# Fused attention and two MLPs on one core: the sum of the last exponential tiles, the scaling, the reciprocals and the first two weights are placed anew

## The chip, the core and the metric

The kernel runs on one core of a Trainium2 chip. Its engines work side by side, each through its own queue in order: TensorE (PE, with its weight loads shown as PEld), VectorE (DVE), ScalarE (ACT), GpSimd (POOL), and SyncE (SP), which here issues loads and stores. The metric is the device time of one execution in microseconds; times of before and after are medians over runs.

## The reference, cut to what matters

```
q_pool = q.reshape(B, H, S // 2, 2, D).mean(axis=3)          # B=2 H=8 S=1152 D=64
scores = matmul(q_pool, k^T) / sqrt(D)
scores = scores - max(scores); attn = exp(scores)
attn   = attn / (sum(attn) + 1e-9)
x = (attn @ v)                      # as 1152 tokens x 512
h = x @ w_in (512 x 2048);  g = relu(h)^2;  y = g @ w_out
out = ((y @ w_a) * (y @ w_b)) @ w_out2                        # 512 x 1536, 512 x 1536, 1536 x 512
```

The weights come as 64-bit words and are taken apart into two float32 parts each (hi and lo), and activations likewise, so that each product of the MLPs is three matmuls (hi hi, hi lo, lo hi).

## The kernel before

The program has a manual schedule: each engine does its instructions in the order in which the code issues them, and only data and buffers make it wait.

**Attention** runs in 16 units (`NU`); unit n is a pair of heads p = n // 2 and half c = n % 2 of its 576 pooled queries, 288 columns (`CQ`). The loop over n (L481) issues for each unit: nine score tiles (`scores`, L365: eight matmuls into a PSUM tile, and an ACT exponential into `e`), and between them, as the letters of `ORDER` say, six steps of the row maxima of the next pair (`max_pair`, L317: a matmul pair into PSUM and a DVE reduction `mm`); behind an odd unit the mixed maxima (`px`) and the negated maxima (`max_end`, `nmw`); the transposes of the pair after that (`prep`, with a copy on ACT to `hi` and the rest on DVE to `lo`); the maxima as a row (`max_row`); then `values` (L399, 36 passes on PE into `po`, copied by ACT to `xf`) and the denominator of the unit before (`denom`, L409: the sums of exponentials `acc` times ones on PE, ACT writes `sg`). Scores, maxima, transposes, values and denominators share four PSUM tiles of two banks (`two_banks`) in turn, so a matmul of the next unit can wait for a DVE reduction to give a tile back.

The sum of a unit's nine exponential tiles: POOL adds tiles 0 to 6 one after the other into `acc` (L382, L384), DVE adds 7 and 8 (`sum_last`, L393), and POOL adds that at the start of the next unit (`sum_end`, L397). Two units later DVE takes the reciprocal of `sg` and scales `xf` by it (`scale`, L426 to L430), both right after the sum of tiles 7 and 8; one unit later ACT and POOL split `xf` (`x_split`, L432) into `xh` and `xl`, the input of the first MLP. The last unit sums its tiles 4 to 8 on DVE (L389).

**Weights** are made in three stages per tile of 512 x 128 (`w_stage`, L121): stage 0 an ACT copy (`wa`) and a DVE operation (L131), stage 1 two DVE operations (L135, L138), stage 2 a subtraction `wlo` (L153) on DVE or, for i from `NE` to 11, on POOL; ACT copies `whi` (L119) before it. Before the change the first `NE` = 4 weights are made in units 12 to 15, three steps in each (L519 to L521), and the first MLP starts with four early tiles (`early_mm`, f = 0 to 3, over the 576 tokens of the first batch, in the PSUM tiles of attention), which lie between the last values and the split of the last unit. Then the other half of the tokens follows for these f in tiles of 288, and f from `NE` on in three tiles of 384 (`mlp1`).

## Time and profile before

| | |
|---|---|
| median of 3 runs | 667.69 us (666.58 to 667.91) |
| profiled execution: its own time / its span | 666.69 us / 664.9 us |
| PE busy | 648.3 us, 98% |
| DVE, ACT, POOL busy | 455.9, 306.2, 203.0 us |
| attention, first values to first tile of the MLP | 30.34 to 234.02 us |
| mean granted clock of TensorE | 0.983 |

Busy shares are over the whole span, and POOL's work lies nearly all in attention, where it is busy nine tenths of the time. Matmuls are pipelined, so a row's duration is longer than the distance to the next; where PE waits is read from its idle time and from the start times. For the attention it helps to cut the span at the first value matmul of each unit, since every unit has the same work in between, but for the maxima (none in units 14 and 15, which have no next pair) and the transposes (none from unit 12 on).

### The profile page before, as it was taken

The page shows a single profiled execution, that of the slowest core. Times are in us where ns is not written, and L with a number is a line of the kernel's source. Part 1 is how long each engine was busy: PE and PEld are TensorE (multiplying, and loading weights), DVE is VectorE, ACT ScalarE, POOL GpSimd, SP SyncE. Part 2 cuts the span into 40 slices and gives each one's busy share as a digit, 9 for nine tenths or more (in the row PEclk, how much of TensorE's full clock was granted, in tenths as well). Part 3 has the DMA queues.
Part 4 walks back from the last instruction along what each step waited for, and adds up shares of the span by engine and source line. Part 5 has one row for each costly group of instructions (what it writes and reads, how often), then busy time and mean ns, then how long its engine had stood idle before and what let it go on. Part 6 is the DMA issues. An engine that isn't in the chain of part 4 may idle for free.

```text
span 664.9 us, 11353 instructions
## 1 busy us (share of the span) xinstructions
PE 648.3 (98%) x4618; PEld 584.5 (88%) x4618; DVE 455.9 (69%) x700; ACT 306.2 (46%) x571; POOL 203.0 (31%) x160
## 2 busy tenths in 40 slices
PE   7999999999979999999999999999999999999997
PEld 5878777777757789999999999999999889999986
DVE  7778988978998898982458855676777112777211
ACT  1546665575554746742356632244554222455100
POOL 1677999999975911310000000000000000000000
PEclk8799999999998999999999999999999999999999
DMA  8704404221041112422333222233434210341022
GB/s 198 159 1 108 100 9 107 53 57 37 4 146 33 47 33 66 126 96 63 96 91 101 94 65 64 64 127 96 128 127 126 65 32 3 125 127 63 18 65 63
DMA packets 55541, 52.90 MB, mean 80 GB/s; under 512 B 20416, under 2 KB 49344, under 8 KB 55488
## 3 DMA queue, kind: packets, MB, share of 16 engines
q1 hardware_dynamic: 55280, 51.58, 27.4%
q8 instruction: 36, 0.59, 0.4%
q10 hardware_dynamic: 208, 0.59, 0.3%
q14 instruction: 17, 0.14, 0.1%
HBM read 49.81 MB, written 2.36 MB: 78 GB/s over the span
## 4 chain that ended last, share of the span: by engine, by line
PE 83%; DVE 12%; ACT 2%; issue 1%; POOL 1%; DVEq 0%; POOLq 0%; ACTq 0%
PE ps L372 9%; PE y L559 5%; PE y L557 5%; PE y L558 5%; PE h L559 4%; PE h L557 4%; PE h L558 4%; PE po L403 4%; PE a L559 4%; PE a L558 4%; PE b L559 4%; PE b L558 4%; PE a L557 4%; PE b L557 4%; PE o L559 4%; PE o L557 4%
## 5 line engine op out<-in xcount | busy, mean ns | idle before, releaser
L384 POOL TENSOR_TENSOR acc<-acc,e 128x576 f32<-128x576 f32 x77 | 113.6, 1475 | 10.2 <-ACT e L377 4.2
L315 DVE TENSOR_REDUCE mm<-pm 128x2 f32<-128x768 f32 x96 | 88.8, 954 | 19.7 <-PE pm L323 19.0
L377 ACT ACTIVATE e<-ps 128x576 f32<-128x576 f32 x144 | 88.3, 656 | 27.7 <-PE ps L372 25.6
L153 DVE TENSOR_TENSOR wlo<-wx,whi 128x512 fp32r<-128x512 f32 x60 | 41.2, 687 | 54.3 <-ACT whi L119 54.2
L403 PE MATMUL po<-e,vin 128*64 128x288 f32 x576 | 73.3, 409 | 0.0
L119 ACT CAST whi<-wx 128x512 fp32r<-128x512 f32 x68 | 42.1, 620 | 64.3 <-DVE wx L138 64.3
L557 PE MATMUL y<-gh,whi 128*128 128x384 f32 x192 | 64.6, 336 | 0.0
L559 PE MATMUL y<-gh,wlo 128*128 128x384 f32 x192 | 64.5, 336 | 0.0
L558 PE MATMUL y<-gl,whi 128*128 128x384 f32 x192 | 64.5, 336 | 0.0
L403 PEld LDWEIGHTS po<-e,vin 128*64 128x64 f32 x576 | 40.0, 137 | 26.4 <-issue 0.2
L559 PE MATMUL h<-xh,wlo 128*128 128x384 f32 (+1 forms) x176 | 57.5, 327 | 0.0
L558 PE MATMUL h<-xl,whi 128*128 128x384 f32 (+1 forms) x176 | 57.5, 327 | 0.0
L557 PE MATMUL h<-xh,whi 128*128 128x384 f32 (+1 forms) x176 | 57.5, 327 | 0.0
L372 PE MATMUL ps<-hi 64*128 64x288 f32 x288 | 48.2, 329 | 6.8 <-DVE mm L315 6.5
L700 DVE TENSOR_TENSOR t<-b,as 128x384 f32<-128x384 f32 x36 | 20.1, 558 | 46.2 <-PE b L559 46.2
L138 DVE SCALAR_TENSOR_TENSOR wx<-raw,wx 128x512 int32<-128x512 int32 x68 | 49.7, 731 | 2.4
L135 DVE SCALAR_TENSOR_TENSOR wx<-wa,wx 128x512 int32<-128x512 int32 x68 | 48.3, 711 | 0.0
L559 PE MATMUL a<-yh,wlo 128*128 128x384 f32 x144 | 48.1, 334 | 0.0
L557 PE MATMUL a<-yh,whi 128*128 128x384 f32 x144 | 48.1, 334 | 0.0
L558 PE MATMUL a<-yl,whi 128*128 128x384 f32 x144 | 48.1, 334 | 0.0
L557 PE MATMUL b<-yh,whi 128*128 128x384 f32 x144 | 48.1, 334 | 0.0
L558 PE MATMUL b<-yl,whi 128*128 128x384 f32 x144 | 48.1, 334 | 0.0
(111 smaller groups left out, 1564.1 us busy)
## 6 DMA issues: line engine op xcount, KB each, us to landing
raw<-in_moe_w_out_dram SPq DMA_DIRECT2D x28, 512.0 KB, 3.4
raw<-in_moe_w_in_dram SPq DMA_DIRECT2D x16, 512.0 KB, 3.8
raw<-in_moe_w_a_dram SPq DMA_DIRECT2D x12, 512.0 KB, 3.5
raw<-in_moe_w_b_dram SPq DMA_DIRECT2D x12, 512.0 KB, 3.6
vin<-in_v_dram SPq DMA_DIRECT2D x8, 576.0 KB, 4.2
qin<-in_q_dram SPq DMA_DIRECT2D x7, 576.0 KB, 5.6
kin<-in_k_dram SPq DMA_DIRECT2D x14, 288.0 KB, 5.8
out_dram<-oacc SPq DMA_DIRECT2D x5, 192.0 KB, 2.2
```

Source lines behind the costliest of these rows:

```text
L119: nc.scalar.copy(w["hi"], w["x"].bitcast(F32))
L135: nc.vector.scalar_tensor_tensor(out=x, in0=a.bitcast(I32), scalar=3, in1=x, op0=ALU.logical_shift_left, op1=ALU.bitwise_or)
L138: nc.vector.scalar_tensor_tensor(out=x, in0=high.bitcast(I32), scalar=-(2 ** 31), in1=x, op0=ALU.bitwise_and, op1=ALU.bitwise_or)
L153: eng.tensor_tensor(out=lo, in0=x.bitcast(F32), in1=hi.bitcast(F32), op=ALU.subtract)
L315: nc.vector.tensor_reduce(out=mm[p][:, i, c], in_=ps, op=ALU.max, axis=AX.X)
L372: nc.tensor.matmul(ps[:, a, :CQ], w, m, start=i == 0, stop=i == 3)
L377: nc.scalar.activation(ex[u, t], ps[:, :, :CQ], AF.Exp, scale=SCALE)
L384: nc.gpsimd.tensor_tensor(out=acc[u], in0=acc[u], in1=ex[u, t], op=ALU.add)
L403: nc.tensor.matmul(po[r, 0, :CQ], vin[u // 2][:, a, t, :], ex[u, t][:, a, :], start=t == 0, stop=t == KT - 1)
L557: nc.tensor.matmul(ps, lh, rh, start=i == 0, stop=False)
L558: nc.tensor.matmul(ps, lh, rl, start=False, stop=False)
L559: nc.tensor.matmul(ps, ll, rh, start=False, stop=i == n - 1)
```

## The change

The DVE sum of tiles 7 and 8 becomes `sum_three`: one DVE reduction over the three tiles 6, 7 and 8, which lie in one buffer, with the tile as the innermost index, 576 words apart. POOL adds only tiles 0 to 5 and then that result. The last unit sums tiles 3 to 5 and 6 to 8 so; for units 14 and 15 the denominator takes `acc` and these sums as matmuls of their own. `scale` is taken apart: `recip` is issued right behind the maxima, ahead of `lo`, and the scaling goes to POOL (to DVE for the last two units). Only two weights (`NE` = 2) are made in attention, by a table `first` that names one step for an even unit from 2 to 14 (two stage-0 steps in unit 2; a stage 0.5 does the first operation of stage 1); unit 15 does stage 0 of weights 2 and 3. Their loads are issued in unit 1. There are two early tiles instead of four, and the denominator of the last unit stands ahead of them.

```diff
...
     xpool = ctx.enter_context(tc.tile_pool(name="xpool", bufs=1))
 
 
-    NE = 4
+    NE = 2
     NW = 5
     NWARM = 32
     HF1 = NF1 // 2
...
         if w is not None:
             nc.scalar.copy(w["hi"], w["x"].bitcast(F32))
 
+    def w_bits(i):
+        w = work[i]
+        if not w.get("bits"):
+            w["bits"] = True
+            nc.vector.scalar_tensor_tensor(
+                out=w["x"], in0=w["a"].bitcast(I32), scalar=3, in1=w["x"], op0=ALU.logical_shift_left, op1=ALU.bitwise_or
+            )
+
     def w_stage(i):
         w = work.setdefault(i, {"stage": 0})
         if w["stage"] == 0:
...
             nc.vector.tensor_scalar(out=x, in0=low, scalar1=float(2.0 ** -29), scalar2=7.0, op0=ALU.mult, op1=ALU.min)
         elif w["stage"] == 1:
             w_hi()
-            a, x, high = w["a"], w["x"], w["high"]
-            nc.vector.scalar_tensor_tensor(
-                out=x, in0=a.bitcast(I32), scalar=3, in1=x, op0=ALU.logical_shift_left, op1=ALU.bitwise_or
-            )
+            w_bits(i)
+            x, high = w["x"], w["high"]
             nc.vector.scalar_tensor_tensor(
                 out=x, in0=high.bitcast(I32), scalar=-(2 ** 31), in1=x, op0=ALU.bitwise_and, op1=ALU.bitwise_or
             )
...
             at["next"] += 1
         w_stage(i)
 
+    def w_next(i, stage):
+
+        if stage == 0.5:
+            return w_bits(i)
+        if stage == 0:
+            at["next"] += 1
+        w_stage(i)
+
     def w_get(key):
         while key not in ready:
             w_step(place[key] + 1)
...
 
             halves = (slice(0, D), slice(D, 2 * D))
             kin, qin, qs, vin, hi, lo, mm, mrow = {}, {}, {}, {}, {}, {}, {}, {}
-            ex, acc, e2, sg, xf = {}, {}, {}, {}, {}
+            ex, e3, acc, e2, sg, xf = {}, {}, {}, {}, {}, {}
 
             def pair(p):
                 b, h = divmod(2 * p, H)
...
                         w, m = (x[p][r, kt], y[p][r, qt]) if x else (onez[r], mrow[u][r])
                         nc.tensor.matmul(ps[:, a, :CQ], w, m, start=i == 0, stop=i == 3)
                 if t % 3 == 0:
-                    e3 = ap.tile([P, 3, 2, CQ], F32, tag="e", bufs=4, name=f"e{u}_{t}")
+                    e3[u, t // 3] = ap.tile([P, 3, 2, CQ], F32, tag="e", bufs=4, name=f"e{u}_{t}")
                     for i in range(3):
-                        ex[u, t + i] = e3[:, i]
+                        ex[u, t + i] = e3[u, t // 3][:, i]
                 nc.scalar.activation(ex[u, t], ps[:, :, :CQ], AF.Exp, scale=SCALE)
-
-                half = 4 if u == NU - 1 else KT - 2
                 if t == 1:
                     acc[u] = ap.tile([P, 2, CQ], F32, tag="acc", bufs=2, name=f"acc{u}")
                     nc.gpsimd.tensor_tensor(out=acc[u], in0=ex[u, 0], in1=ex[u, 1], op=ALU.add)
-                elif 1 < t < half:
+                elif 1 < t < KT - 3 * extra(u):
                     nc.gpsimd.tensor_tensor(out=acc[u], in0=acc[u], in1=ex[u, t], op=ALU.add)
-                elif u == NU - 1 and t > half:
-                    if t == half + 1:
-                        e2[u] = ap.tile([P, 2, CQ], F32, tag="e2", bufs=2, name=f"e2_{u}")
-                    x = ex[u, half] if t == half + 1 else e2[u]
-                    nc.vector.tensor_tensor(out=e2[u], in0=x, in1=ex[u, t], op=ALU.add)
-
-            def sum_last(u):
-                e2[u] = ap.tile([P, 2, CQ], F32, tag="e2", bufs=2, name=f"e2_{u}")
-                nc.vector.tensor_tensor(out=e2[u], in0=ex[u, KT - 2], in1=ex[u, KT - 1], op=ALU.add)
+
+            def extra(u):
+
+                return 1 if u < NU - 1 else 2
+
+            def sum_three(u, g):
+
+                e2[u, g] = ap.tile([P, 2, CQ], F32, tag="e2", bufs=3, name=f"e2_{u}_{g}")
+                nc.vector.tensor_reduce(
+                    out=e2[u, g].rearrange("p a q -> p (a q)"), in_=e3[u, g].rearrange("p t a q -> p (a q) t"),
+                    op=ALU.add, axis=AX.X,
+                )
 
             def sum_end(u):
-                if u >= 0:
-                    nc.gpsimd.tensor_tensor(out=acc[u], in0=acc[u], in1=e2[u], op=ALU.add)
+                if 0 <= u < NU - 2:
+                    for g in range(3 - extra(u), 3):
+                        nc.gpsimd.tensor_tensor(out=acc[u], in0=acc[u], in1=e2[u, g], op=ALU.add)
 
             def values(u):
                 po = two_banks(f"po{u}")
...
                 if not 0 <= u < NU:
                     return
                 pt = two_banks(f"den{u}")[:, 0]
-                sums = [acc[u], e2[u]] if u == NU - 1 else [acc[u]]
+                sums = [acc[u]] + [e2[u, g] for g in range(3 - extra(u), 3) if u >= NU - 2]
                 for i, x in enumerate(sums):
                     for a, r in enumerate(halves):
                         nc.tensor.matmul(pt[r, :CQ], ones, x[:, a, :], start=i == 0, stop=i == len(sums) - 1)
...
                 sl = slice(b * SQ + c * CQ, b * SQ + (c + 1) * CQ)
                 return xh[:, hs.start // 2, sl], xl[:, hs.start // 2, sl]
 
-            def scale(u):
-                if not 0 <= u < NU:
-                    return
-                nc.vector.reciprocal(sg[u], sg[u])
-                nc.vector.tensor_tensor(out=xf[u], in0=xf[u], in1=sg[u], op=ALU.mult)
+            def recip(u):
+                if 0 <= u < NU:
+                    nc.vector.reciprocal(sg[u], sg[u])
+
+            def scale(u, eng=None):
+                if 0 <= u < NU:
+                    (eng or nc.gpsimd).tensor_tensor(out=xf[u], in0=xf[u], in1=sg[u], op=ALU.mult)
 
             def x_split(u):
                 if 0 <= u < NU:
...
             gpool = None
 
             ORDER, BUSY = "MSMSSMSMSSMSSMS", "MSMSMSMSMSMSMSMSMS"
+
+            first = {2: ((0, 0), (1, 0)), 4: ((0, 0.5),), 6: ((0, 1),), 8: ((1, 0.5),), 10: ((1, 1),), 12: ((0, 2),), 14: ((1, 2),),
+                     15: ((NE, 0), (NE + 1, 0))}
             for n in range(NU):
                 p, odd = divmod(n, 2)
 
...
                 else:
                     todo = [(p + 1, 2 * odd + j, c) for j in range(2) for c in range(MX)] if p + 1 < NPR else []
                 sum_end(n - 1)
+                if n == 1:
+                    w_load(3)
                 if not odd:
                     q_sum(p + 2)
                     load_k(p + 3)
                     load_q(p + 3)
                 else:
                     load_v(p + 2)
-                if n == NU - 1:
-                    scale(n - 2)
                 t = 0
                 for step in BUSY if n == 1 else ORDER:
                     if step == "S":
                         scores(n, t)
                         t += 1
+                        if n == NU - 1 and t == 2:
+                            recip(n - 2)
+                        if n == NU - 1 and t == 6:
+                            sum_three(n, 1)
                     elif todo:
                         max_pair(*todo.pop(0))
                         if odd and len(todo) == 3:
...
                 if (odd or not n) and m < NPR:
                     max_mix(m)
                     max_end(m, 1)
+                if n < NU - 1:
+                    recip(n - 2)
                 if p + 2 < NPR:
                     prep(p + 2, odd)()
                 if n:
                     max_row(n + 1)
                 if n < NU - 1:
-                    sum_last(n)
-                x_split(n - 3)
-                if n >= NU - 4:
-                    for _ in range(3):
-                        w_step(NE)
-                end = n == NU - 1
-                if end:
+                    sum_three(n, 2)
+                    scale(n - 2)
+                    x_split(n - 3)
+                    for step in first.get(n, ()):
+                        w_next(*step)
+                    values(n)
                     denom(n - 1)
-                values(n)
-                scale(n - 1 if end else n - 2)
-                if not end:
+                else:
+                    sum_three(n, 2)
                     denom(n - 1)
+                    recip(n - 1)
+                    scale(n - 2)
+                    values(n)
+                    denom(n)
+                    scale(n - 1, nc.vector)
+                    for u in (n - 3, n - 2, n - 1):
+                        x_split(u)
+                    for step in first[n]:
+                        w_next(*step)
                 if not n:
                     max_row(1)
             qk_stack.close()
             gpool = gs.enter_context(tc.tile_pool(name="gpool", bufs=1, side="right", reuse_waits="tile"))
             early_mm(ps_s, 0)
-            denom(NU - 1)
-            x_split(NU - 3)
-            x_split(NU - 2)
             early_mm(ps_s, 1)
-            scale(NU - 1)
+            recip(NU - 1)
+            scale(NU - 1, nc.vector)
+            x_split(NU - 1)
+            w_next(NE, 1)
             early_post(gpool, 0)
-            x_split(NU - 1)
-            for f in range(2, NE):
-                early_mm(ps_s, f)
-                early_post(gpool, f - 1)
-            early_post(gpool, NE - 1)
+            w_next(NE, 2)
+            early_post(gpool, 1)
             return gpool
 
     def rest(lo, x, hi):
```

On DVE, from the last maximum of unit 12 (`mm`<-`pm_1_2`) to the first of unit 13 (`pm_2_0`). Before:

```order
L315 TENSOR_REDUCE mm_2512<-pm_1_2_2623 128x2
L393 TENSOR_TENSOR e_12_2643<-e_6_2610 128x576
L131 TENSOR_SCALAR wx_2651<-raw_2647 128x512
L131 TENSOR_SCALAR wx_2657<-raw_2653 128x512
L135 SCALAR_TENSOR_TENSOR wx_2651<-wa_2649,wx_2651 128x512
L138 SCALAR_TENSOR_TENSOR wx_2651<-raw_2647,wx_2651 128x512
L429 RECIPROCAL sg_2509<-sg_2509 128x288
L430 TENSOR_TENSOR xf_2312<-xf_2312,sg_2509 128x288
L315 TENSOR_REDUCE mm_2512<-pm_2_0_2696 128x2
```

After:

```order
L329 TENSOR_REDUCE mm_2527<-pm_1_2_2637 128x2
L444 RECIPROCAL sg_2524<-sg_2524 128x288
L405 TENSOR_REDUCE e_12_2_2658<-e_6_2625 128x576
L159 TENSOR_TENSOR wlo_1564<-wx_809,whi_1563 128x512
L329 TENSOR_REDUCE mm_2527<-pm_2_0_2691 128x2
```

Four weight operations and the scaling are gone from this place, one subtraction of an earlier weight has come, and the reciprocal stands ahead of the sum.

On DVE, from the mixed maxima behind an odd unit (5) to the first maximum of the next. Before:

```order
L315 TENSOR_REDUCE mm_1028<-px_2_1336 128x1
L344 TENSOR_REDUCE nmw_94<-mm_1028 128x2
L344 TENSOR_REDUCE nmw_94<-mm_1028 64x1 x2
L295 TENSOR_TENSOR lo_1155<-pt_1_1342,hi_1154 128x416
L295 TENSOR_TENSOR lo_1155<-pt_1_1342,hi_1154 128x288
L393 TENSOR_TENSOR e_5_1362<-e_6_1305 128x576
L429 RECIPROCAL sg_1202<-sg_1202 128x288
L430 TENSOR_TENSOR xf_1011<-xf_1011,sg_1202 128x288
L315 TENSOR_REDUCE mm_1402<-pm_0_0_1403 128x2
```

After:

```order
L329 TENSOR_REDUCE mm_1038<-px_2_1345 128x1
L358 TENSOR_REDUCE nmw_94<-mm_1038 128x2
L358 TENSOR_REDUCE nmw_94<-mm_1038 64x1 x2
L444 RECIPROCAL sg_1212<-sg_1212 128x288
L309 TENSOR_TENSOR lo_1165<-pt_1_1352,hi_1164 128x416
L309 TENSOR_TENSOR lo_1165<-pt_1_1352,hi_1164 128x288
L405 TENSOR_REDUCE e_5_2_1372<-e_6_1315 128x576
L329 TENSOR_REDUCE mm_1411<-pm_0_0_1412 128x2
```

The reciprocal moved ahead of the two `lo`, the reduction stands for the sum, and the scaling is gone.

On ACT, from the last exponential of unit 15 to the first early tiles' `r`. Before:

```order
L377 ACTIVATE e_6_3112<-ps_8_3126 128x576
L435 CAST xh<-xf_2686 128x288
L119 CAST whi_3002<-wx_2992 128x512
L119 CAST whi_3144<-wx_2996 128x512
L418 ACTIVATE sg_3152<-den_3149,eps 128x288
L407 COPY xf_3173<-po_3154 128x288
L418 ACTIVATE sg_3211<-den_3206,eps 128x288
L435 CAST xh<-xf_2870 128x288
L435 CAST xh<-xf_3023 128x288
L576 ACTIVATE r_0_0_3246<-e_3181 128x576
```

After:

```order
L391 ACTIVATE e_6_3080<-ps_8_3092 128x576
L434 ACTIVATE sg_3109<-den_3104,eps 128x288
L423 COPY xf_3132<-po_3113 128x288
L434 ACTIVATE sg_3141<-den_3134,eps 128x288
L453 CAST xh<-xf_2683 128x288
L453 CAST xh<-xf_2856 128x288
L453 CAST xh<-xf_2996 128x288
L137 ACTIVATE wa_3150<-raw_454 128x512
L137 ACTIVATE wa_3154<-raw_1561 128x512
L453 CAST xh<-xf_3132 128x288
L607 ACTIVATE r_0_0_3224<-e_3162 128x576
```

The two weight copies (`whi`) that stood ahead of the sums `sg` are gone from there, and stage 0 of two weights (`wa`) stands behind them.

## Rows read from the trace of the kernel before

**Rows 1.** The page, part 1: busy time of the engines over the whole span.

```profile
PE 648.3 (98%) x4618; PEld 584.5 (88%) x4618; DVE 455.9 (69%) x700; ACT 306.2 (46%) x571; POOL 203.0 (31%) x160
```

**Rows 2.** Stretches: length; busy us (count) of PE, PEld, DVE, ACT, POOL; clock; DMA.

```profile
71.04:84.58 13.54, 12.89 (x138) 9.96 (x139) 11.83 (x15) 7.95 (x16) 13.09 (x11) 1.00 0.58 133
...
84.58:97.76 13.18, 13.15 (x140) 10.08 (x139) 10.98 (x13) 8.12 (x15) 11.76 (x9) 1.00 0.00 1
...
97.76:110.38 12.62, 12.62 (x135) 9.86 (x136) 10.82 (x15) 7.81 (x16) 12.17 (x11) 1.00 0.61 140
...
110.38:124.13 13.75, 13.39 (x138) 10.13 (x138) 11.84 (x13) 8.22 (x15) 13.13 (x11) 1.00 0.01 3
...
176.96:189.41 12.45, 11.98 (x129) 9.04 (x128) 11.54 (x15) 7.41 (x15) 10.46 (x10) 1.00 0.53 170
...
189.41:208.48 19.07, 14.81 (x132) 12.07 (x131) 15.75 (x16) 8.70 (x16) 14.10 (x10) 0.82 0.10 32
```

**Rows 3.** Timeline of DVE, 189 to 200.5: start, time, line, tiles, idle before.

```profile
190.87 3.17 DVE L131 TENSOR_SCALAR wx<-raw 128x512 int32<-128x512 uint32 x2
...
193.96 1.28 DVE L135 SCALAR_TENSOR_TENSOR wx<-wa,wx 128x512 int32<-128x512 int32 x1
...
195.28 1.79 DVE L138 SCALAR_TENSOR_TENSOR wx<-raw,wx 128x512 int32<-128x512 int32 x1
...
197.00 1.94 DVE L429 RECIPROCAL sg<-sg 128x288 f32<-128x288 f32 x1
...
199.34 1.82 DVE L315 TENSOR_REDUCE mm<-pm 128x2 f32<-128x768 f32 x2
```

**Rows 4.** Timeline of PE, 199 to 206.6.

```profile
200.35 0.61 PE L372 MATMUL ps<-hi 64*128 64x288 f32 x2 [4.26 <-DVE mm L315]
...
205.56 0.44 PE L372 MATMUL ps<-hi,lo 64*128 64x288 f32 x2
...
205.99 0.29 PE L372 MATMUL ps<-mrow,onez 64*128 64x288 f32 x2
```

**Rows 5.** Timeline of DVE at the ends of units 4 and 9.

```profile
85.41 1.22 DVE L295 TENSOR_TENSOR lo<-pt,hi 128x1024 fp32r<-128x1024 f32 x1 [1.64 <-ACT hi L291]
...
90.00 1.82 DVE L315 TENSOR_REDUCE mm<-pm 128x2 f32<-128x768 f32 x2 [0.34 <-PE pm L323]
...
151.35 0.96 DVE L295 TENSOR_TENSOR lo<-pt,hi 128x416 fp32r<-128x416 f32 x2
...
156.06 0.96 DVE L315 TENSOR_REDUCE mm<-pm 128x2 f32<-128x768 f32 x1 [0.17 <-PE pm L323]
```

**Rows 6.** Groups by shape, whole span: count, busy us, mean ns, idle before.

```profile
L384 POOL TENSOR_TENSOR acc<-acc,e 128x576 f32<-128x576 f32 x77 | 113.6, 1475 | 10.2 <-ACT e L377 4.2
...
L315 DVE TENSOR_REDUCE mm<-pm 128x2 f32<-128x768 f32 x96 | 88.8, 954 | 19.7 <-PE pm L323 19.0
...
L315 DVE TENSOR_REDUCE mm<-px 128x1 f32<-128x384 f32 x8 | 4.4, 547 | 0.0
...
L344 DVE TENSOR_REDUCE nmw<-mm 128x6 fp32r<-128x18 f32 x8 | 1.4, 174 | 0.3
...
L344 DVE TENSOR_REDUCE nmw<-mm 128x2 fp32r<-128x6 f32 x8 | 1.2, 151 | 0.0
...
L393 DVE TENSOR_TENSOR e<-e 128x576 f32<-128x576 f32 x15 | 18.3, 1219 | 2.4 <-ACT e L377 2.4
```

**Rows 7.** Timeline of PE, 237.3 to 240.3.

```profile
237.92 0.66 PE L416 MATMUL den<-e,ones 128*64 128x288 f32 x4
...
239.82 0.40 PE L557 MATMUL e<-xh,whi 128*128 128x288 f32 x1 [1.25 <-ACT sg L418]
```

**Rows 8.** Timeline of ACT, 228 to 245.

```profile
238.75 0.62 ACT L119 CAST whi<-wx 128x512 fp32r<-128x512 f32 x1 [7.30 <-DVE wx L138]
...
239.67 0.39 ACT L407 COPY xf<-po 128x288 f32<-128x288 f32 x1
...
242.82 0.65 ACT L576 ACTIVATE r<-e 128x576 f32<-128x576 f32 x1
```


## The prediction, made before the changed kernel ran

> **What bounds the kernel now.** I read the busy times first: TensorE (PE) is busy for 648.3 of 664.9 us [rows 1], so only about 16 us can be won without taking work away from it. Then I cut the attention into its sixteen units (a pair of heads and half of its queries each) at the start of their 36 value matmuls and asked for busy time per stretch [rows 2]. A unit with a full set of maxima takes 13.18 us when it goes from an even to an odd unit and 12.62 us from odd to even, at best. Others of the same content take longer: three even ones 13.52, 13.75 and 13.74 (one row stands for them), two odd ones 13.54 and 13.30, and one stretch of 12.45 has PE idle for 0.47. One stands out: 189.41 to 208.48, 19.07 us with a mean clock of 0.82.
>
> Then the waits. In that stretch PE's scores sit idle for 4.26 us, released by a VectorE (DVE) maximum [rows 4]. DVE was late because between two rounds of maxima it did, in a row, the sum of two exponential tiles, four steps on the first weights (3.17, 1.28, 1.79 us), a reciprocal of 1.94 and a scaling, and began the next maximum at 199.34 [rows 3]. [...] The smaller excesses of the other units are the same queue, without the weights: the DVE work at the boundary of two units decides when the first maximum of the next unit gives its PSUM slot back. Last I read the end of attention: PE's last denominator starts at 237.92, the next first-layer matmul at 239.82, waiting for ScalarE's (ACT) sum tile [rows 7], and ACT reached that tile and the copy of the last values at 239.67 only because a weight copy stood ahead and waited for DVE [rows 8].
>
> **The change part by part.**
>
> *The reduction.* The sum of tiles 7 and 8 (mean 1219 ns) gives way to one reduction over three tiles, 1728 elements in, 576 out [rows 6]. No row has a reduction from SBUF of that length. Nearest are the maxima: 954 ns for two rows of 384 elements and 547 for one [rows 6], so 1.06 ns per element and 0.14 fixed: 0.14 + 1728 x 1.06 = 1.97 us. The far end comes from the reductions with short rows: 18 elements in six results take 174 ns, six in two results 151, so 1.92 ns per element, and 0.15 + 1722 x 1.92 = 3.46 us. The new one has rows of three, as these, but its length is that of the maxima, and in these tiny ones nearly all is fixed cost, a difference of 23 ns between groups. I take 1.97 and keep 3.46 for the range. No reduction here shows less than 1.06 ns per element, so 1.83 is the least.
>
> The three elements of a row lie 576 words apart. [...] No row of this trace has such a stride.
>
> *Boundary of two units.* The reciprocal goes ahead of the split of the transposed keys (lo), the scaling to GpSimd (POOL). Behind an even unit lo waits for ACT anyway, so the reciprocal fills that gap. In the best even unit lo starts at 85.41 and takes 1.22, and the next maximum waits for PE until 90.00: from lo's end DVE has 3.37 us [rows 5]. Now it needs 1.97 and, in units 4 to 10, one weight step, 0.7 to 1.9 (of rows 3's kind): 2.7 to 3.9, so 0 to 0.5 late, 0.15 in the mean. Behind an odd unit it has 156.06 less 151.35, where lo begins right behind the negated maxima, so 4.71 [rows 5]. Now it needs reciprocal 1.94 [rows 3], lo 0.96, reduction 1.97, together 4.87: 0.16 late. So the known excess, (0.34 + 0.57 + 0.56) + (0.92 + 0.68) + 0.47 = 3.5 us, shrinks to about 5 x 0.15 + 4 x 0.15, and unit 2, which takes two first steps of weights (0.8 if they find POOL idle, 3.17 as in rows 3), is 0 to 1.8 late; I take 0.6. Together 1.9, so **1.6 us gained**.
>
> *POOL* loses one addition per unit (1475 ns [rows 6]) and gains the scaling, two inputs with half of its elements: 0.74 us, at most the 1475 of the whole. It was busy for 11.76 to 13.13 us of these units [rows 2], so it gets up to 0.7 freer and is no worse off at worst: nothing counted. Were the scaling dearer than that, the sums for the denominators would come late.
>
> *The weights.* Unit 12 keeps one step (a subtraction, 0.7 to 1.5) where rows 3 show 6.24 us of steps. So the idle 4.26 goes, and with it the slow clock: 5.45 us at half the level cost 2.7. Of these 7.0 I leave 0.5 for the step that stays: **6.5 us gained**. The first three weight loads go out in unit 1, ahead of a value load on SP's queue which is needed three units later; the DMA share is low there. Weights 2 and 3 are finished only behind attention, with their subtractions on POOL, which idles there: twice 1.28 + 1.79 us on DVE, or 6.1 (less, since those of rows 3 stood beside a busy POOL), in place of two reciprocals (3.9) and the two subtractions. The eight tiles of f = 0 and 1 cover them; without that cover PE would wait for weight 2, by up to its 3.1.
>
> *End of attention.* The last two units' sums are no longer added on POOL, so two denominators have one more pair of matmuls each, four passes in at most 0.66 [rows 7], of which I take 0.5, as the last ones run out beside the next work: **1.0 lost**. The wait from 237.92 + 0.5 to 239.82 goes, since no weight copy stands ahead of the sums on ACT: **1.4 gained**. But with two early tiles instead of four the next pool's first bank is that of the second early tile, and its first matmul must wait until ACT has read it: 0.65 [rows 8] and a hand-over of 0.1, **0.75 lost**; before, two more tiles hid this. Processing f = 2 and 3 in tiles of 384 columns instead of 288 is the same number of columns: nothing counted.
>
> Sum: 6.5 + 1.6 + 1.4 - 1.0 - 0.75 = 7.75 us. The profiled execution took 666.69 us (span 664.9 and 1.8 around it), 1.0 below the median of 667.69, inside the runs' 666.58 to 667.91. 666.69 - 7.75 = 658.9, and I say **659.0**.
>
> **Rivals.**
>
> *The reduction is slow, and DVE becomes the bound* (the other side). Each boundary of units 2 to 12, eleven of them, has its room used up at 1.97 us, so each further microsecond of the reduction costs about 11. At 3.46 us that is 16: **675**. The gain is gone at 1.97 + 7.75 / 11 = 2.7 us; beyond it the kernel is slower than before. For it: rows of three are the shape of the dearer rows [rows 6]. Against it: the length, and that the maxima keep their rate however busy POOL is. [...]
>
> *A smaller stall takes the place of the large one.* Unit 2 with its two first steps is the place: 1.97 + 3.17 against 3.37 is 1.8 us of idle PE, and if the clock falls behind it as behind the 4.26, 2.7 more, against 0.6 counted: 3.9 more, **662.8**. Against: idle times of up to half a microsecond in rows 2's slow units left the clock at 1.00.
>
> *The change does not do what it says:* the weights come in time but the boundaries stay as late as now, because the reduction takes up what the sum and the scaling leave free (1.97 in; 1.22 [rows 6] and a scaling out). Then 1.6 is not gained: 660.5, inside the forecast's range.
>
> **How the numbers follow.** Forecast 0.57 (655.5 to 662.5, the last rival in it), the smaller stall and its like 0.17 (662.5 to 665.3), no change 0.05, the slow reduction 0.21 (668 to 676, as it is nearer to one end or the other). Within 0.2% (1.3 us) is about what a measurement of this kernel can't tell from no change. So faster 0.74, same 0.05, slower 0.21. The range reaches from 655.5 (all boundaries free, no new wait at the end) into the slow case to 672.
>
> **What would show it.** The reduction's mean: near 1.97 or above 2.7 decides. The stretch that was 19.07 should be near 12.6 with clock 1.00; even and odd units near 13.2 and 12.6; no PE wait for ACT at the end but one of 0.7 before the third group of first-layer matmuls. A stretch behind unit 2 much above 13.5 would be the smaller stall. The forecast is wrong if DVE is the releaser of PE in most units.

## The result, and the profile after

The changed kernel takes 656.35 us (median of four runs, 655.81 to 657.44) where the kernel before takes 667.76; the ratio is 0.9835, with a 95% interval of 0.9817 to 0.9853. The forecast was 659.0. The profiled execution has a span of 654.9 us, 10.0 less than before. The first part of the page of the changed kernel, busy time by engine, answers to [rows 1]:

```profile
PE 645.5 (99%) x4602; PEld 582.3 (89%) x4602; DVE 450.5 (69%) x682; ACT 306.7 (47%) x571; POOL 185.5 (28%) x159
```

TensorE's idle time went from about 16.6 to 9.4 us; POOL lost 17.5 us of work, DVE 5.4. Where the 10.0 us come from is read from the starts of the value matmuls and of the two stages of the first multilayer part (`e`: the early tiles, `y`: its output):

| stretch | before, us | after, us | gained, us | forecast, us |
|---|---|---|---|---|
| start to unit 0's values | 30.3 | 30.4 | -0.1 | 0 |
| unit 0's values to unit 12's | 159.1 | 156.3 | 2.8 | 1.6 |
| unit 12's values to unit 13's | 19.07 | 12.58 | 6.5 | 6.5 |
| unit 13's values to unit 14's | 10.56 | 10.40 | 0.2 | 0 |
| unit 14's values to the first `y` | 68.1 | 67.2 | 0.9 | -0.35 |
| first `y` to the end | 377.8 | 378.0 | -0.3 | 0 |

The stretches of the changed kernel, as [rows 2] had them of before (length; busy us and count of PE, PEld, DVE, ACT, POOL; clock; DMA). They begin at the values of units 2, 4, 5, 12, 14 and 15:

```profile
57.65:71.44 13.79, 13.38 (x139) 10.12 (x138) 12.79 (x14) 9.04 (x16) 10.42 (x9) 1.00 0.01 3
...
84.08:97.30 13.22, 13.19 (x139) 10.12 (x138) 11.66 (x13) 8.17 (x15) 12.32 (x10) 1.00 0.02 5
97.30:109.95 12.65, 12.65 (x137) 9.87 (x136) 11.76 (x15) 7.87 (x16) 10.36 (x11) 1.00 0.60 140
...
186.71:199.29 12.58, 12.54 (x131) 9.52 (x130) 11.21 (x12) 7.41 (x14) 11.14 (x10) 1.00 0.01 1
...
209.69:220.69 11.00, 11.00 (x121) 8.22 (x122) 6.36 (x4) 7.50 (x15) 9.54 (x8) 1.00 0.01 1
220.69:226.61 5.92, 5.92 (x50) 3.30 (x46) 5.52 (x6) 0.90 (x2) 0.00 (x0) 1.00 0.00 0
```

PE's busy time is now the whole stretch, to within 0.04 us, in all of these but unit 2's. Every even unit from 4 to 10 takes 13.2 and every odd one from 3 to 9 12.65, which were the best cases before. The clock is 1.00 in all of them. Two groups by shape, whole span, answer to [rows 6] (count, busy us, mean ns, idle before):

```profile
L405 DVE TENSOR_REDUCE e<-e 128x576 f32<-128x1728 f32 x17 | 35.9, 2119 | 4.9 <-ACT e L391 4.9
```

```profile
L448 POOL TENSOR_TENSOR xf<-xf,sg 128x288 f32<-128x288 f32 x14 | 11.2, 798 | 5.6 <-DVE sg L444 5.6
```

The reduction takes 2.12 us (1.97 was forecast), the scaling on POOL 0.80 (0.74). DVE at the end of unit 4, and then of unit 9, by its timeline (start, time, line, tiles, idle before); [rows 5] are the same places before:

```profile
85.12 1.16 DVE L309 TENSOR_TENSOR lo<-pt,hi 128x1024 fp32r<-128x1024 f32 x1
86.20 2.12 DVE L405 TENSOR_REDUCE e<-e 128x576 f32<-128x1728 f32 x1
88.25 0.74 DVE L125 SCALAR_TENSOR_TENSOR wx<-wa,wx 128x512 int32<-128x512 int32 x1
89.57 1.82 DVE L329 TENSOR_REDUCE mm<-pm 128x2 f32<-128x768 f32 x2 [0.58 <-PE pm L337]
...
149.80 1.95 DVE L444 RECIPROCAL sg<-sg 128x288 f32<-128x288 f32 x1
151.67 0.89 DVE L309 TENSOR_TENSOR lo<-pt,hi 128x416 fp32r<-128x416 f32 x2
152.47 2.13 DVE L405 TENSOR_REDUCE e<-e 128x576 f32<-128x1728 f32 x1
154.51 1.82 DVE L329 TENSOR_REDUCE mm<-pm 128x2 f32<-128x768 f32 x2
```

Behind the even unit DVE is done 0.58 us before PE has the next maximum's data. Behind the odd one it goes from step to step without a gap and begins the maximum 4.71 us after the reciprocal began, which is exactly the room that [rows 5] gave. Each step starts some 0.08 us before the row of the step ahead of it ends (151.67 against 149.80 + 1.95).

At the end of attention the forecast had a new wait: the first 288-column tile behind the two early ones was to wait until ACT had read the second early tile. PE's and then ACT's timeline:

```profile
233.07 0.29 PE L588 MATMUL h<-xh,whi 128*128 128x288 f32 x1
```

```profile
233.27 0.65 ACT L607 ACTIVATE r<-e 128x576 f32<-128x576 f32 x1
```

PE begins that tile with no idle time, 0.85 us before ACT has read the early one. The wait does not exist.

### The profile page after: what moved, and what is told of

The parts are those of the page before. It is cut to its first block, busy times and chain, and to the rows that moved or that the text cites. A ratio compares the mean times of both kernels' runs of the same rounds, so it can differ in the third digit from the quotient of the medians.

```text
span 654.9 us, 11288 instructions
## 1 busy us (share of the span) xinstructions
PE 645.5 (99%) x4602; PEld 582.3 (89%) x4602; DVE 450.5 (69%) x682; ACT 306.7 (47%) x571; POOL 185.5 (28%) x159
## 4 chain that ended last, share of the span: by engine, by line
PE 96%; DVE 3%; ACT 0%; issue 0%; POOL 0%; POOLq 0%
PE ps L386 12%; PE po L419 10%; PE y L590 5%; PE y L588 5%; PE y L589 5%; PE h L590 5%; PE h L589 5%; PE h L588 5%; PE a L590 4%; PE b L590 4%; PE a L589 4%; PE b L589 4%; PE a L588 4%; PE b L588 4%; PE o L590 4%; PE o L589 4%
## 5 line engine op out<-in xcount | busy, mean ns | idle before, releaser
L329 DVE TENSOR_REDUCE mm<-pm 128x2 f32<-128x768 f32 x96 | 88.8, 953 | 17.5 <-PE pm L337 16.9
L396 POOL TENSOR_TENSOR acc<-acc,e 128x576 f32<-128x576 f32 x61 | 86.9, 1425 | 4.8
L589 PE MATMUL h<-xl,whi 128*128 128x384 f32 (+1 forms) x184 | 60.9, 331 | 0.0
L590 PE MATMUL h<-xh,wlo 128*128 128x384 f32 (+1 forms) x184 | 60.9, 331 | 0.0
L588 PE MATMUL h<-xh,whi 128*128 128x384 f32 (+1 forms) x184 | 60.8, 331 | 0.0
L144 DVE SCALAR_TENSOR_TENSOR wx<-raw,wx 128x512 int32<-128x512 int32 x68 | 47.2, 693 | 2.3
L590 PE MATMUL b<-yh,wlo 128*128 128x384 f32 x144 | 48.1, 334 | 0.0
```

The costliest lines, as they stand in the source:

```text
L144: nc.vector.scalar_tensor_tensor(out=x, in0=high.bitcast(I32), scalar=-(2 ** 31), in1=x, op0=ALU.bitwise_and, op1=ALU.bitwise_or)
L329: nc.vector.tensor_reduce(out=mm[p][:, i, c], in_=ps, op=ALU.max, axis=AX.X)
L396: nc.gpsimd.tensor_tensor(out=acc[u], in0=acc[u], in1=ex[u, t], op=ALU.add)
L588: nc.tensor.matmul(ps, lh, rh, start=i == 0, stop=False)
L589: nc.tensor.matmul(ps, lh, rl, start=False, stop=False)
L590: nc.tensor.matmul(ps, ll, rh, start=False, stop=i == n - 1)
```

## The experiments

The stretch from the start to unit 0's values takes 28.6 to 31.3 us in the profiles of this study, in nearly the same code (30.4 and 31.1 in two executions of the changed kernel). So traces are compared from unit 0's values on; the medians hold that scatter. Each ratio is to the kernel before as it ran beside that kernel (medians 666.87 to 667.76).

| kernel | median, us | ratio to before (95%) | unit 0's values to the end, us |
|---|---|---|---|
| before | 667.76 | 1 | 634.6 |
| after | 656.35 | 0.9835 (0.9817 to 0.9853) | 624.5 |
| after, again | 657.38 | 0.9850 (0.9829 to 0.9872) | 624.6 |
| weights back | 662.21 | 0.9925 (0.9905 to 0.9946) | 628.9 |
| scaling on DVE | 662.24 | 0.9929 (0.9911 to 0.9948) | 630.4 |
| reciprocal late | 661.67 | 0.9924 (0.9901 to 0.9946) | 629.3 |
| sum of two tiles | 658.94 | 0.9879 (0.9862 to 0.9896) | 625.8 |
| two additions | 657.94 | 0.9868 (0.9847 to 0.9888) | 626.1 |
| reduction twice | 678.53 | 1.0172 (1.0141 to 1.0202) | 644.9 |
| before, weights spread | 676.00 | 1.0127 (1.0087 to 1.0168) | 642.0 |
| before, reduction | 676.87 | 1.0158 (1.0132 to 1.0184) | 641.4 |
| no double step, POOL's sums | 655.42 | 0.9838 (0.9819 to 0.9856) | 623.0 |

### Weights back behind units 12 and 13

```
-            first = {2: ((0, 0), (1, 0)), 4: ((0, 0.5),), 6: ((0, 1),), 8: ((1, 0.5),), 10: ((1, 1),), 12: ((0, 2),), 14: ((1, 2),),
+            first = {12: ((0, 0), (1, 0), (0, 1)), 13: ((1, 1), (0, 2), (1, 2)),
                      15: ((NE, 0), (NE + 1, 0))}
```

> The changed kernel, with the six steps of weights 0 and 1 put back behind units 12 and 13, three each. If the stall of the kernel before came from the weight steps in DVE's queue: unit 12 to 13 goes back from 12.6 to about 19 us, with PE idle for about 4 us and a granted clock near 0.8 in that stretch, the other units stay at 13.2 and 12.65 (unit 2 gets 0.5 shorter), and the time is 656.4 + 6.5 - 0.5 = 662 to 663 us. If it was the whole queue (the scaling and the reciprocal too) and the steps alone fit: 656 to 658 us.

The time was as expected, 662.2, but not its form. Stretches of units 12 and 13, one row of DVE's timeline, and PE's two rows with idle time:

```profile
186.87:201.61 14.74, 12.76 (x131) 9.55 (x130) 13.72 (x15) 8.61 (x16) 11.80 (x10) 1.00 0.12 37
201.61:214.73 13.12, 10.68 (x118) 8.03 (x116) 10.93 (x12) 6.57 (x14) 7.45 (x7) 1.00 0.14 41
```

```profile
190.72 2.56 DVE L139 TENSOR_SCALAR wx<-raw 128x512 int32<-128x512 uint32 x2
```

```profile
195.53 0.40 PE L386 MATMUL ps<-hi 64*128 64x288 f32 x2 [1.97 <-DVE mm L329]
...
210.38 0.40 PE L386 MATMUL ps<-hi 64*128 64x288 f32 x2 [2.44 <-ACT xf L423]
```

Unit 12 loses 2.16 us and not 6.5: the same four weight steps that took 3.17, 1.28 and 1.79 in [rows 3] took 2.56, 0.68 and 0.69 here. In the kernel before each of the four began while POOL was in the middle of an addition or a subtraction; here POOL was idle when the last two began. PE was idle for 1.97, and the clock stayed at 1.00 behind that. Unit 13 lost 2.71 with its own three steps, PE waiting there for ACT's copy of the values, which stood behind a weight copy (`whi`) that waited for the weight step on DVE (1.78 us from 207.60 on). In the changed kernel the move of the weights is thus worth 4.4 us (628.9 less 624.5), the 0.56 that it costs in unit 2 taken off; of the 6.5 that unit 12 lost before, 2.16 come back with the steps alone. The rest goes with a shorter idle time (1.97 for 4.26) and a clock that did not fall; which part of DVE's emptier queue shortened the idle time was not taken apart.

### The scaling back on DVE

```
-                    scale(n - 2)
+                    scale(n - 2, nc.vector)
```

> The changed kernel, with the scaling back on DVE behind the reduction. DVE gets 0.46 to 0.75 us more at every boundary. Behind even units it now waits 0.58 us for PE, behind odd ones not at all. Theory one, a DVE that begins late makes PE late at once: six odd boundaries x 0.6 and a little at the even ones, 659 to 660.5 us. Rival, PE has work ahead that hides about a microsecond at the odd boundaries: 656 to 657 us.

Slower than either theory: 5.9 us lost on the trace. Units 4 and 5; then two rows of DVE and one of POOL at the end of unit 4; then POOL at the same place of the changed kernel:

```profile
84.91:98.97 14.06, 13.38 (x138) 10.12 (x137) 13.07 (x14) 8.20 (x15) 11.74 (x10) 1.00 0.01 2
98.97:111.97 13.00, 12.80 (x136) 9.82 (x135) 12.12 (x16) 7.88 (x16) 9.23 (x9) 1.00 0.60 137
```

```profile
89.05 0.45 DVE L448 TENSOR_TENSOR xf<-xf,sg 128x288 f32<-128x288 f32 x1
89.41 1.91 DVE L125 SCALAR_TENSOR_TENSOR wx<-wa,wx 128x512 int32<-128x512 int32 x1
```

```profile
89.28 1.49 POOL L413 TENSOR_TENSOR acc<-acc,e 128x576 f32<-128x576 f32 x1 [0.25 <-DVE e L405]
```

```profile
88.40 1.25 POOL L455 TENSOR_TENSOR xl<-xf,xh 128x288 fp32r<-128x288 f32 x1
```

The odd unit lost 0.35 for the 0.45 of scaling: there is little room there. The even one lost 0.84, though it had 0.58 to spare: the weight step behind the scaling took 1.91 instead of 0.74. It started 0.13 us after POOL's addition of two tiles. In the changed kernel the step starts at 88.25, ahead of POOL's subtraction at 88.40, and there it is POOL's that is stretched (1.25, against 0.80 at the same place here). So in both places, of two operations that each read two tensors from SBUF, the one that started second was stretched. The reduction, with one input, kept its time (2.05 to 2.15 us, below). But one input is no safeguard by itself: the first weight step has one, and behind unit 2 of the changed kernel the second of the two such steps began 0.10 us behind an addition of POOL and took 1.65 us, where the first took 0.42:

```profile
62.13 1.65 DVE L139 TENSOR_SCALAR wx<-raw 128x512 int32<-128x512 uint32 x1
```

```profile
62.03 1.47 POOL L413 TENSOR_TENSOR acc<-acc,e 128x576 f32<-128x576 f32 x1 [1.38 <-DVE e L405]
```

Why that step was stretched and the reduction was not, no run here shows.

### The reciprocal behind the reduction

```
-                if n < NU - 1:
-                    recip(n - 2)
                 if p + 2 < NPR:
                     prep(p + 2, odd)()
...
                     sum_three(n, 2)
+                    recip(n - 2)
                     scale(n - 2)
```

> The changed kernel, with the reciprocal behind the reduction, as before, instead of behind the maxima. Behind an even unit DVE then waits again for ACT ahead of the key split (1.64 us in the kernel before) and does 2.05 + 1.94 + 0.7 us from there to the next maximum, where PE allows 3.3: 1.4 late at six boundaries, even units 14.5 instead of 13.2, 663 to 665 us; odd units unchanged at 12.65. Rival, the order doesn't matter since the amount of DVE's work is the same: 656 to 657 us.

The first theory held, a little smaller. Units 4 and 5, and DVE's `lo` at the end of unit 4:

```profile
84.33:98.55 14.22, 13.38 (x139) 10.12 (x138) 12.34 (x13) 8.26 (x15) 12.87 (x11) 1.00 0.09 27
98.55:111.20 12.65, 12.65 (x137) 9.87 (x136) 11.03 (x14) 7.89 (x16) 9.66 (x10) 1.00 0.50 116
```

```profile
85.23 1.23 DVE L309 TENSOR_TENSOR lo<-pt,hi 128x1024 fp32r<-128x1024 f32 x1 [1.65 <-ACT hi L305]
```

The idle 1.65 us ahead of `lo` are back, even units take 1.0 more, odd ones nothing. The order costs 4.8 us without any change in the work.

### The sum of two tiles, and two additions

In the first kernel POOL adds the third tile again for units 0 to 14, in the second DVE adds all three.

```
-                elif 1 < t < KT - 3 * extra(u):
+                elif 1 < t < (KT - 2 if u < NU - 1 else KT - 6):
...
+                if u < NU - 1:
+                    return nc.vector.tensor_tensor(out=e2[u, g], in0=ex[u, KT - 2], in1=ex[u, KT - 1], op=ALU.add)
                 nc.vector.tensor_reduce(
```

> The changed kernel, with DVE adding only the last two exponential tiles as before, and POOL the third. POOL was busy for 12.32 us of an even unit of 13.22 and 10.36 of an odd one of 12.65; an addition is 1.43 more. Theory one, POOL has room over a pair of units (25.6 of 25.9) and DVE only gets 0.9 freer: 655.5 to 657 us, unit 2 a little shorter. Rival, the reduction is needed to keep POOL from becoming the bound, since its late additions hold the exponential tiles and its late scaling the values: 0.5 us per even unit and more, 659 us or above.

Unit 2's stretch and the one wait that is new, with who was waited for (us in total, times, longest):

```profile
58.57:71.80 13.23, 13.21 (x139) 10.14 (x138) 12.09 (x14) 8.94 (x16) 12.01 (x9) 1.00 0.01 2
```

```profile
PE den L434 <- POOL acc L396: 1.5, 1, 1.5
```

POOL had room in nearly all units, which stay at 13.2 and 12.65 (one took 13.43), and unit 2 got 0.56 shorter. What was lost (1.3 us on the trace) is one wait of 1.5 in unit 15, where the denominator of unit 14 found POOL's sums late. So both theories missed the end: between units 2 and 12 the reduction is not needed, as the first had it, but at the last denominators the work that it takes from POOL counts.

```
-                nc.vector.tensor_reduce(
-                    out=e2[u, g].rearrange("p a q -> p (a q)"), in_=e3[u, g].rearrange("p t a q -> p (a q) t"),
-                    op=ALU.add, axis=AX.X,
-                )
+                nc.vector.tensor_tensor(out=e2[u, g], in0=ex[u, 3 * g], in1=ex[u, 3 * g + 1], op=ALU.add)
+                nc.vector.tensor_tensor(out=e2[u, g], in0=e2[u, g], in1=ex[u, 3 * g + 2], op=ALU.add)
```

> The changed kernel, with two additions of two tiles each on DVE in place of one reduction over three. Alone an addition takes 0.75 us, beside POOL's work up to 1.8 in the rows seen so far, where the reduction always took 2.05 to 2.15. If DVE's steps with two inputs are slowed by POOL: two additions take 2.4 us in the mean, from 1.5 to 3.4, and some boundaries come late: 657 to 661 us. If not: 1.5 each time, DVE 0.6 freer, 656 us and unit 2 down to 13.2.

The two groups of additions, whole span:

```profile
L406 DVE TENSOR_TENSOR e<-e,e 128x576 f32<-128x576 f32 x17 | 22.3, 1314 | 0.9
L405 DVE TENSOR_TENSOR e<-e 128x576 f32<-128x576 f32 x17 | 16.4, 965 | 3.9 <-ACT e L391 3.9
```

An addition alone takes 0.76 us (measured with POOL idle, below), so a pair would be 1.5; in this place it took 1.31 + 0.97 = 2.28, more than the reduction's 2.12. Even units came to 13.6, and 1.6 us were lost on the trace. The medians of this kernel and of the changed one beside it, 657.94 and 657.38, do not tell them apart. The reduction's times lie between 2.05 and 2.15 in all 17 cases, whatever POOL did; the sum of two tiles of the kernel before took between 0.75 and 1.80.

### The reduction twice

```
-                nc.vector.tensor_reduce(
+                for _ in range(2 if u < NU - 1 else 1):
+                    nc.vector.tensor_reduce(
```

> The changed kernel, with every reduction of units 0 to 14 done twice into the same tile: 4.24 us of DVE per unit instead of 2.12. By the price of the slow-reduction rival (11 us per microsecond, from a point of 0 to 0.6 us above the time that it has now): six odd boundaries x 2.05 and six even ones x 1.5, 21 us, 677 us, more if the granted clock falls behind the idle times. If PE has about a microsecond hidden at each boundary: 665 to 668 us.

Units 4 and 5:

```profile
89.89:104.57 14.68, 13.37 (x139) 10.11 (x138) 13.67 (x14) 8.24 (x15) 13.03 (x11) 1.00 0.01 2
104.57:119.09 14.52, 13.29 (x137) 9.99 (x136) 13.80 (x16) 8.01 (x16) 9.48 (x10) 1.00 0.51 123
```

The rival's price was right. For 2.12 us more the even unit lost 1.46 and the odd one 1.87, so the room left is 0.66 and 0.25; 20.4 us in all on the trace, at an unchanged clock. Of these 18.3 lie between the values of unit 2 and those of unit 13; units 0 and 1 and the first MLP, which the price had not counted, lost 2.4, and the rest was 0.3 shorter.

### The kernel before, with one part alone

```
-                if n >= NU - 4:
-                    for _ in range(3):
-                        w_step(NE)
+                if 2 <= n < NU - 2:
+                    w_step(NE)
...
+                if n == 1:
+                    w_load(3)
```

> The kernel before, with its twelve first weight steps made one behind each of units 2 to 13, instead of three behind each of units 12 to 15; nothing else of the change. If the room that the other edits made on DVE is needed: the stall of 6.5 us behind unit 12 goes, but steps of 0.45 to 1.4 us, 10.2 in all, come to boundaries that are already 0.3 to 0.6 us late: about 667 to 671 us, so no gain. If spreading alone brings the gain: 661 us.

Worse than expected: 1.3% slower than the kernel before, 7.3 us on the trace. Units 4 and 5, a weight step of DVE behind unit 4, and PE's idle time there:

```profile
85.50:103.47 17.97, 14.57 (x138) 11.73 (x137) 14.95 (x15) 8.28 (x15) 13.99 (x10) 0.91 0.10 30
103.47:119.68 16.21, 14.34 (x137) 11.42 (x136) 13.09 (x17) 8.50 (x17) 14.26 (x12) 0.89 0.59 143
```

```profile
88.20 1.90 DVE L135 SCALAR_TENSOR_TENSOR wx<-wa,wx 128x512 int32<-128x512 int32 x1
```

```profile
95.58 0.41 PE L372 MATMUL ps<-hi 64*128 64x288 f32 x2 [3.40 <-DVE mm L315]
```

Unit 12 was cured (12.59 us), but behind units 4, 5 and 10 the stall came back, with the two steps with two inputs at 1.90 and 1.17 beside POOL (0.73 and 1.17 behind unit 5), the scaling behind them at 1.46 for 0.46, and the granted clock down to 0.91 and 0.89 in those stretches. PE's only idle time in the second of them was shorter than in the first:

```profile
112.01 0.40 PE L372 MATMUL ps<-hi 64*128 64x288 f32 x2 [1.87 <-DVE mm L315]
```

Without room on DVE this spreading makes one stall into three. It is not the change's own schedule, which has eight pieces, of two weights, all behind even units, where this has twelve whole steps behind even and odd ones; that schedule in the kernel before was not run.

```
-                nc.vector.tensor_tensor(out=e2[u], in0=ex[u, KT - 2], in1=ex[u, KT - 1], op=ALU.add)
+                nc.vector.tensor_reduce(
+                    out=e2[u].rearrange("p a q -> p (a q)"), in_=e3[u, 2].rearrange("p t a q -> p (a q) t"),
+                    op=ALU.add, axis=AX.X,
+                )
...
-                half = 4 if u == NU - 1 else KT - 2
+                half = 4 if u == NU - 1 else KT - 3
```

> The kernel before, with the reduction over three tiles in place of the sum of two, and POOL's addition of the third left out; nothing else of the change. DVE gets 2.12 - 1.22 = 0.9 us more at each boundary, which are already late: 11 x 0.9, about 677 us. If POOL's additions held the boundaries (it gets 1.43 us freer per unit): 666 us or below.

As expected, 676.9. Its units 2 to 10 take 14.2 when even and 14.4 when odd, where before had 13.2 to 13.8 and 12.6 to 13.5. So neither of the two large edits, tried so, is a gain on the kernel before. That the scaling on POOL and the reciprocal's new place make the room that they use fits the 5.9 and 4.8 us that their loss costs in the changed kernel; the kernel before with these two alone was not run.

### What a reduction over strided tiles costs

In two kernels reductions of several shapes stand ahead of the second multilayer stage, three of each; no row of POOL stands in that stretch.

```
+                nc.vector.tensor_reduce(out=one[:, :576], in_=yf[:, :1728].rearrange("p (t q) -> p q t", t=3), op=ALU.add, axis=AX.X)
+                nc.vector.tensor_reduce(out=one[:, :576], in_=yf[:, :1728].rearrange("p (q t) -> p q t", t=3), op=ALU.add, axis=AX.X)
+                nc.vector.tensor_reduce(out=one[:, :3], in_=yf[:, :1728].rearrange("p (t q) -> p t q", t=3), op=ALU.add, axis=AX.X)
+                nc.vector.tensor_reduce(out=one[:, :288], in_=yf[:, :1728].rearrange("p (t q) -> p q t", t=6), op=ALU.add, axis=AX.X)
+                nc.vector.tensor_reduce(out=one[:, :288], in_=yf[:, :864].rearrange("p (t q) -> p q t", t=3), op=ALU.add, axis=AX.X)
+                nc.vector.tensor_tensor(out=one[:, :576], in0=yf[:, :576], in1=yf[:, 576:1152], op=ALU.add)
```

> The changed kernel, with five forms of reduction and one sum of two tiles put in three times each ahead of the second multilayer stage, where DVE is mostly idle; they write a tile that nothing reads. If the reduction's 2.12 us come from the stride of 576 words: the same 1728 elements with the three of a row side by side take 1.97 us or less, and three rows of 576 too. If they come from the short rows: both orders with rows of three take 2.1, rows of six less, three long rows about 1.9. If from neither, all take the same 2.1 us for 1728 elements, and 864 elements half.

The groups (L715 to L720 are the six lines above in their order; the time of the whole kernel is not used):

```profile
L718 DVE TENSOR_REDUCE probe<-yh 128x288 f32<-128x1728 f32 x3 | 9.4, 3149 | 0.1
...
L715 DVE TENSOR_REDUCE probe<-yh 128x576 f32<-128x1728 f32 x3 | 6.4, 2132 | 0.1
L716 DVE TENSOR_REDUCE probe<-yh 128x576 f32<-128x1728 f32 x3 | 5.9, 1953 | 0.1
L717 DVE TENSOR_REDUCE probe<-yh 128x3 f32<-128x1728 f32 x3 | 5.9, 1953 | 0.1
L719 DVE TENSOR_REDUCE probe<-yh 128x288 f32<-128x864 f32 x3 | 3.4, 1144 | 0.1
...
L720 DVE TENSOR_TENSOR probe<-yh 128x576 f32<-128x576 f32 x3 | 2.3, 758 | 0.1
```

Short rows cost nothing: three side by side and three long rows both take 1.95, what the forecast's line through the maxima gives (1.97). The stride of the kernel's form costs 0.18 more. Six tiles in a row, though, take 3.15 for the same number of elements. The second kernel asked what decides that:

```
+                nc.vector.tensor_reduce(out=one[:, :288], in_=yf[:, :576].rearrange("p (t q) -> p q t", t=2), op=ALU.add, axis=AX.X)
...
+                nc.vector.tensor_reduce(out=one[:, :432], in_=yf[:, :1728].rearrange("p (t q) -> p q t", t=4), op=ALU.add, axis=AX.X)
```

> The changed kernel, with reductions over 2, 3, 4, 5 and 6 tiles of 288 elements, 6 tiles of 96 and 4 tiles of 432, three of each, ahead of the second multilayer stage; they write a tile that nothing reads. With 0.14 us fixed, three tiles so far took 1.15 to 1.16 ns per element (576 and 288 elements in a tile) and six of 288 took 1.74. If the number of places visited in turn decides: 2 and 3 tiles at 1.05 to 1.16, and from 4 or 5 on 1.74, for 96 and 432 elements in a tile as well. If an even number is what costs: 2, 4 and 6 at 1.74, 3 and 5 at 1.16. If the distance decides, 4 tiles of 432 and 6 of 96 differ from those of 288.

L715 is two tiles of 288, L717 and L718 four and five of them, L720 six of 96, L721 four of 432 (three and six of 288 took 1143 and 3134 ns, as in the first kernel):

```profile
L721 DVE TENSOR_REDUCE probe<-yh 128x432 f32<-128x1728 f32 x3 | 9.3, 3084 | 0.1
L718 DVE TENSOR_REDUCE probe<-yh 128x288 f32<-128x1440 f32 x3 | 7.9, 2649 | 0.1
L717 DVE TENSOR_REDUCE probe<-yh 128x288 f32<-128x1152 f32 x3 | 6.5, 2152 | 0.1
L720 DVE TENSOR_REDUCE probe<-yh 128x96 f32<-128x576 f32 x3 | 3.4, 1149 | 0.1
...
L715 DVE TENSOR_REDUCE probe<-yh 128x288 f32<-128x576 f32 x3 | 2.3, 762 | 0.1
```

Less the fixed 0.14 us, an element costs 1.08 ns with two tiles, 1.16 with three, and 1.70 to 1.75 with four, five and six, at 96, 288 and 432 elements in a tile. So it is the number of tiles visited in turn, and neither an even count nor, between 96 and 576 words, the distance. Three is the last cheap one.

### Two edits more: no double step, and POOL's sums at the end

```
-            first = {2: ((0, 0), (1, 0)), 4: ((0, 0.5),), 6: ((0, 1),), 8: ((1, 0.5),), 10: ((1, 1),), 12: ((0, 2),), 14: ((1, 2),),
+            first = {2: ((0, 0),), 4: ((1, 0),), 6: ((0, 0.5),), 8: ((0, 1),), 10: ((1, 0.5),), 12: ((1, 1),), 13: ((0, 2),), 14: ((1, 2),),
...
-                if 0 <= u < NU - 2:
+                if 0 <= u < NU - 1:
...
-                sums = [acc[u]] + [e2[u, g] for g in range(3 - extra(u), 3) if u >= NU - 2]
+                sums = [acc[u]] + [e2[u, g] for g in range(2, 3) if u == NU - 1]
...
+                    nc.gpsimd.tensor_tensor(out=acc[n], in0=acc[n], in1=e2[n, 1], op=ALU.add)
                     sum_three(n, 2)
                     denom(n - 1)
```

> The changed kernel with two edits: no unit takes two weight steps (stage 0 of weight 1 behind unit 4, the later steps one place on, the first subtraction behind unit 13), and POOL adds the reduced tiles of unit 14 and the first of unit 15 into the sums, so that both denominators lose a pair of matmuls. Expected if unit 2's excess is the second step and the four passes per denominator lie on PE's path: unit 2 to 3 goes from 13.79 to 13.2, unit 14 to 15 from 11.00 to 10.5, unit 15 to the first early tile from 5.92 to 5.45; 1.5 us in all, so 654.9 where the changed kernel has 656.4. Rival: the subtraction behind unit 13 or POOL's two additions make a denominator wait, as the addition of unit 14 did for 1.5 us in the kernel with the sum of two tiles: 656 to 658.

> The changed kernel as it is, beside the others on the same chip: 656.4 us, a ratio to the kernel before of 0.983 to 0.985.

The stretches of units 2, 14 and 15:

```profile
55.85:69.07 13.22, 13.22 (x138) 10.19 (x138) 11.32 (x13) 8.35 (x15) 9.90 (x8) 1.00 0.01 3
207.37:217.88 10.51, 10.51 (x117) 7.93 (x118) 5.88 (x4) 7.14 (x15) 10.14 (x8) 1.00 0.01 2
217.88:223.31 5.43, 5.43 (x46) 3.01 (x42) 5.40 (x5) 1.13 (x3) 2.17 (x2) 1.00 0.00 0
```

All three came out as worked out: 0.57 + 0.49 + 0.49, 1.5 us on the trace (623.0 against 624.5 and 624.6). In time it is 655.42 against 657.38 on the same chip; the two intervals to the kernel before overlap, so the medians alone do not show a gain; the trace does.

## Why the prediction was right, and where its steps were not

- **Where the time was, and the sign: right.** PE was the bound, DVE's queue at the boundaries and behind unit 12 was what kept it waiting, and the 19.07 us became 12.58 at clock 1.00. The term of 6.5 measured 6.5, in part by luck: PE's busy time in that stretch fell from 14.81 to 12.54, so the slow clock had cost 2.3 and not 2.7 (in the kernel before the granted clock was 0.50 from 200.35 to 205.80, the 5.45 us of the forecast, and 1.00 from 206.00 to 207.40; matmul pairs start 0.24 us apart in the first stretch and 0.13 in the second, so not quite twice), and the 0.5 that I left for the step that stays was not lost.
- **What the 6.5 is: partly wrong.** I put it down to the weight steps and to the clock that fell behind them. With the steps back in the changed kernel unit 12 lost 2.16 and unit 13 2.71, with no fall of the clock; three of the four steps in [rows 3] took 1.63, 1.28 and 1.79 us beside POOL's work, and 0.99, 0.68 and 0.69 in that run, where POOL was done sooner. The stall before was the steps, their slow execution, the rest of the queue and the clock together.
- **Boundaries: mis-sized, 2.8 instead of 1.6.** I left 1.9 us of lateness at the boundaries: 0.6 in unit 2, the rest over nine others. Unit 2's measured 0.57 (13.79 less 13.22), at clock 1.00, so the smaller stall of the rivals did not come: of its two first steps only one was slow. The rest was nought. Two sizes did that: the weight steps behind units 4 to 10 took 0.72 to 0.78, the low end of the 0.7 to 1.9 that I had averaged, and the rows' times overlap by 0.08 from step to step, so that the odd boundary's 4.87 was 4.7.
- **End of attention: wrong by two terms.** The two pairs of extra matmuls cost 0.98 (unit 14's stretch 10.51 to 11.00, and the last kernel takes 0.49 back in each place): 1.0 was forecast. The wait ahead of the second early tile is gone: 1.25 idle in [rows 7], and 1.3 by the kernel before with the reduction, where the first early tile runs to the second in 4.49 instead of 5.80. The 0.75 of a new wait were not paid. The step that failed is "the next pool's first bank is that of the second early tile"; PE started there while ACT had not begun to read that tile. Which bank it was given I did not trace. And tiles of 384 columns are a little cheaper than those of 288, which I had counted at nothing: the four of 288 that begin at 233.07 end at 239.44, 6.37 us for 48 matmuls, where the same number of columns takes 6.24 in tiles of 384 (37.45 us for six weights). The early tiles are dearer still: the 96 matmuls of the four take 13.01 us before, without the denominator between them, the 48 of the two 6.46 after, so the pair that is gone cost 6.55. For the two weights that changed over that makes 6.55 + 6.37 - 2 x 6.24, or 0.44. The sum of these, 1.3 - 1.0 + 0.44, is 0.7 to 0.8 of the 0.9; another 0.1 lies in the last unit's values, whose 36 passes run for 4.37 instead of 4.47. Both misses, at the boundaries and at the end, went the same way: 1.2 and 1.25 us, about the 2.65 between forecast and result.
- **The reduction: right within its bounds.** 2.12 against 1.97; the 0.15 are the stride, which cost 0.18 in the run with several shapes. Two or three tiles, at 1.08 and 1.16 ns per element, stay near the 1.06 of the maxima; from four to six it was 1.70 to 1.75. That three tiles lie on the cheap side of that border the forecast had from no row; the runs showed it.
- **The slow-reduction rival: its mechanism is real.** Twice the time cost 18.3 us at the eleven boundaries of units 2 to 12, 8.6 for each microsecond where I had said 11, because 0.66 and 0.25 of room were left, and 20.4 in all. The kernel would be level with before at some 3.2 us by a straight line (2.12 + 10.0 / 9.6, the 9.6 being 20.4 / 2.12) and some 3.5 if the room goes first (6 x (x - 0.66) + 5 x (x - 0.25) = 10.0 at x = 1.4 more), both estimates from these rows, and not at 2.7.
- **POOL:** forecast as no worse off. It was busy for 12.32 instead of 11.76 us of unit 4 and for 10.36 instead of 12.17 of unit 5. The sum of two tiles shows where it counts: at the last denominators alone.

## What to carry to other kernels

When one engine's queue sets when buffers come free, moving a burst of its work into other places pays only where those places have room: here a spreading of the burst and the longer reduction, each alone, made the kernel before 1.3 and 1.6% slower, and in the changed kernel the two small edits (another engine for the scaling, the reciprocal into a gap that waited anyway) were worth 5.9 and 4.8 us. Read the room of each place from the trace, as the time from the last fixed point to the next step that must not be late, start to start. A step's own time is not fixed: here weight steps on DVE took more than twice as long (1.91 for 0.74, 1.65 for 0.42) where POOL had just started an operation.
